# First MLP layer streams 32 instead of 64 columns per matmul; the useless matmuls of the layer norm become 512 columns wide

## The chip, the cores and the metric

The kernel runs on one core of a Trainium2 chip. The metric is the device time of one execution in microseconds (us); medians over executions are quoted.

PE is the matmul engine (PEld its weight loads), DVE the vector engine, ACT the scalar engine, SP the engine that issues most transfers, PSUM the memory that matmuls write to.

## The reference, cut to what matters

It is one decode step for 8 sequences: a modulated layer norm, attention over a cache of 8192 keys and values for 8 key/value heads, an output projection, then a second layer norm and an MLP. Only the part after the projection matters here:

```python
x = x + ga * attention(h, k_cache, v_cache, wq, wo)
h = _layernorm(x) * (1 + cb) + sb
hid = relu(h @ w1 + b1) ** 2          # 8 x 512 by 512 x 1792: "layer one"
x = x + gb * (hid @ w2 + b2)          # 8 x 1792 by 1792 x 512: "layer two"
```

## The kernel before: the parts that the change touches

Activations are held transposed, 128 features on the partitions and 8 sequences in the columns, so a matmul has only 8 useful columns. The kernel repeats them eight times (`wide`), 64 columns, so that PE has more to stream, and it puts matmuls of an identity matrix, whose result nobody reads, where PE would wait ("useless matmuls"). Neither touches the result; I take both to be there for the granted clock of PE, which in this kernel's trace is 1.0 or 0.5 of full speed. Full speed counts: back-to-back matmuls of 128 columns start 56 ns apart at 1.0 and 107 at 0.5.

```python
def pe_fill(n, at=7):                       # n useless matmuls of 128 columns
    for _ in range(n):
        op("tensor", lambda e: e.matmul(bank(at)[:, 0:128], IDENT[:, :], IDENT[:, :]))
def pe_stream(n, at):                       # n useless matmuls of 512 columns
    rhs = IDENT[:, :].unsqueeze(1).to_broadcast([128, 4, 128])
    for _ in range(n):
        op("tensor", lambda e: e.matmul(bank(at).rearrange("p (a r) -> p a r", a=4), IDENT[:, :], rhs))
# ... (cut: attention) ...
# the second weight matrix, 14 row tiles of 128, in two transfers: 12 tiles (1536 KB) and 2
d_w2 = [dma("sync", s_w2[i], lambda e, a=a, z=z, j=j: e.dma_start(
    W2v[:, a:z, :].rearrange("p (k j) n -> p k (j n)", j=j),
    B_w2[128 * a:128 * z].rearrange("(k p j) n -> p k (j n)", p=128, j=j)))
    for i, (a, z, j) in enumerate(((0, F2, 4), (F2, FT, 2)))]
# ... (cut) ...
# x1T is ready; mean by matmul, transposes of x1, then
pe_fill(4, 7)
# ... (cut: difference, squares, sum on DVE; variance by matmul; square root on ACT; h on DVE) ...
pe_fill(14, 7)
wcol = lambda k, f: fcol(W1v[:, k, :], f)   # every 4th column of W1 (every 2nd in the last two tiles)
for ks in (range(KT - 1), range(KT - 1, KT)):
    for f in range(FT):                     # layer one: 14 x 4 = 56 matmuls
        for k in ks:
            t = op("tensor", lambda e, f=f, k=k: e.matmul(
                hT_w[f // 7][:, f % 7, :, :], wcol(k, f), wide(hbT[:, k, :]), start=False, ...),
                [k_hb, d_w1[k // (KT - 1)]])
        # ... (cut: after f = 6 and f = 13, DVE: relu, square -> k_sq) ...
for f in range(FT):                         # layer two: 14 x 2 = 28 matmuls of 256 columns
    if f == F2:                             # F2 = 12
        pe_fill(6, 7)
    for cc in range(2):
        t = op("tensor", lambda e, f=f, cc=cc: e.matmul(
            yN_ps[64 * cc:64 * cc + B, :], hidT[:, f, :], W2v[:, f, 256 * cc:256 * (cc + 1)], ...),
            [k_sq[f // 7], d_w2[0 if f < F2 else 1]])
# ... (cut: two DVE operations, output) ...
```

## Time and profile before

672.04 us (median of 3, 671.46 to 672.15); the profiled execution took 671.61. The page of the profiled execution gives what bounds the kernel as a whole:

```profile
DMA  9999999999999999999999999999999999999995
...
HBM read 283.66 MB, written 0.01 MB: 423 GB/s over the span
```

The transfers are busy until the last 40th of the span: the kernel is bound by what it reads. Its tail, after the last values have landed at 656.50 us, is where the change lies. Here is the tail on PE, from the timeline: start in us, duration in us, engine, line, operation, output<-inputs, shapes, count; in brackets how long the engine was idle before, and whom it waited for.

```profile
657.48 0.96 PE L659 MATMUL PS<-oTn,wo_sb 128*128 128x8 bf16 x32 [0.29 <-DVE oTn L654]
...
659.95 0.39 PE L684 MATMUL PS<-sqs,ONESM 128*128 128x8 f32 x2 [0.21 <-DVE sqs L682]
660.19 1.04 PE L433 MATMUL PS<-IDENT 128*128 128x128 bf16 x14
661.38 3.12 PE L696 MATMUL PS<-hbT,ring 128*128 128x64 bf16 x56
664.82 1.48 PE L713 MATMUL PS<-ring,hidT 128*8 128x256 bf16 x24 [0.32 <-DVE KTb L702]
```

L632 is the last product with the values, L659 the last piece of the output projection, L684 the variance, L433 the useless matmuls, L696 layer one, L713 layer two. The chain that ended last, in order of time (start, duration, what):

```profile
656.55 0.66 PE PS L632 x16
...
661.38 2.81 PE PS L696 x49
...
664.47 0.22 DVE hidT L704
...
664.83 1.47 PE PS L713 x24
666.30 0.44 PE PS L433 x6
666.74 0.33 PE PS L713 x4
```

So layer one, ReLU, layer two, the six useless matmuls and the last four follow each other without a gap. The view of stretches gives the granted clock of PE in the first number after the groups (PEclk; then the DMA share and GB/s):

```profile
core 0: us, PE busy (x) PEld busy (x) DVE busy (x) ACT busy (x) POOL busy (x), PEclk, DMA share, GB/s
661.40:664.20 2.80, 2.80 (x53) 2.80 (x54) 0.00 (x0) 0.00 (x0) 0.00 (x0) 0.50 0.53 208
664.80:667.00 2.20, 2.18 (x34) 1.48 (x34) 0.23 (x2) 0.00 (x0) 0.00 (x0) 1.00 0.00 0
```

Layer one ran at half clock (0.50), 53 ns from start to start, layer two at full clock (1.00), 109 ns from one pair of matmuls to the next. The clock records of the trace have these two values alone and, from 36.25 us on, 37 switches between them, each a whole multiple of 3.41 us after the one before. The last two before the end of layer two are at 660.89 us, to half, and at 664.30, back to full. A "window" below is one such stretch of 3.41 us between two possible switches. And a last line, from the list of transfers (size in KB, us from issue to landing):

```profile
ring<-in_B_w_dram SPq DMA_DIRECT2D x1, 1536.0 KB, 24.5
```

This is the large part of the second weight matrix, issued at 640.14 us. The landing records of the trace show its 16 parts arriving from 660.96 to 664.69 us. Layer two needs all of them; `hidT`, its other input, was ready at 664.47 + 0.22 = 664.69 us.

### The profile page before, as it was taken

To read this page: it belongs to the slowest core of one execution; us is meant where nothing else is said; L and a number is where in the kernel's file an instruction comes from. 1 tells how busy PE (TensorE), PEld (TensorE's weight loads), DVE (VectorE), ACT (ScalarE), POOL (GpSimd) and SP (SyncE) were. 2 spreads that over 40 slices of the span, in tenths; PEclk is the share of its full clock that TensorE was granted. 3 is DMA by queue.
4 is the path that set the end of the run, shared out by engine and by line. 5 is a ranking of instruction groups with operands and counts; after the bars stand their busy time and mean duration, and the time that the engine had idled before them with its cause. 6 is when DMAs were issued, how large, how long until landed. Compare 5 with 4: busy or idle time off the path is not lost.

```text
span 669.9 us, 16178 instructions
## 1 busy us (share of the span) xinstructions
PE 496.0 (74%) x7486; PEld 342.4 (51%) x7486; DVE 299.4 (45%) x568; ACT 235.5 (35%) x281; POOL 17.2 (3%) x67
## 2 busy tenths in 40 slices
PE   2295964799639983699648995499836996489976
PEld 2283731676218751477317761287415763177644
DVE  2162741467216661267315671166503673156722
ACT  2052630466006640166204660066302652046600
POOL 7200000000000000000000000000000000000000
PEclk9996996799869997599958997699977999789998
DMA  9999999999999999999999999999999999999995
GB/s 373 435 399 434 429 425 436 433 427 434 430 436 430 425 432 434 436 430 427 430 436 432 429 431 429 436 434 427 432 429 438 433 429 425 434 438 434 425 412 235
DMA packets 12938, 283.96 MB, mean 424 GB/s; under 512 B 1234, under 2 KB 2291, under 8 KB 4340
## 3 DMA queue, kind: packets, MB, share of 16 engines
q1 hardware_dynamic: 12868, 283.65, 98.9%
q8 instruction: 13, 0.21, 0.1%
q14 instruction: 9, 0.07, 0.0%
q10 hardware_dynamic: 48, 0.02, 0.0%
HBM read 283.66 MB, written 0.01 MB: 423 GB/s over the span
## 4 chain that ended last, share of the span: by engine, by line
PE 50%; DMA 41%; DVE 5%; ACT 2%; issue 1%; SPq 0%
DMA ring<-in_A_k_cache_dram 37%; PE PS L447 36%; PE PS L462 9%; DMA ring<-in_A_v_cache_dram 4%; DVE Pm L552 3%; PE PS L580 2%; ACT KTb L452 1%; ACT P_sb L530 1%; DVE m L467 1%; PE PS L539 1%; PE PS L438 0%; PE PS L559 0%; PE PS L696 0%; PE PS L713 0%; DVE rhs_r L556 0%
## 5 line engine op out<-in xcount | busy, mean ns | idle before, releaser
L452 ACT ACTIVATE KTb<-PS 128x1024 bf16<-128x1024 bf16 x192 | 196.8, 1025 | 376.3 <-PE PS L447 376.3
L447 PE MATMUL PS<-IDENT,ring 128*128 128x128 bf16 x4096 | 266.4, 227 | 51.6 <-DMA ring<-in_A_k_cache_dram 43.7
L447 PEld LDWEIGHTS PS<-IDENT,ring 128*128 128x128 bf16 x4096 | 245.8, 102 | 100.4 <-DMA ring<-in_A_k_cache_dram 44.8
L454 DVE COPY KTb<-PS 128x1024 bf16<-128x1024 bf16 x320 | 209.9, 688 | 150.3 <-PE PS L447 148.3
L580 PE MATMUL PS<-ring,Pm 128*32 128x512 bf16 x992 | 81.1, 485 | 64.5 <-DMA ring<-in_A_v_cache_dram 63.6
L589 DVE CAST O_sb<-PS 128x512 bf16<-128x512 f32 x31 | 21.4, 692 | 144.0 <-PE PS L580 144.0
L462 PE MATMUL PS<-KTb,Qb 128*32 128x512 bf16 x1024 | 79.2, 386 | 4.5 <-ACT KTb L452 4.5
L580 PEld LDWEIGHTS PS<-ring,Pm 128*32 128x32 bf16 x992 | 29.2, 115 | 101.8 <-DMA ring<-in_A_v_cache_dram 65.0
L438 PE MATMUL PS<-IDENT 128*128 128x512 bf16 x120 | 31.3, 380 | 0.0
L530 ACT ACTIVATE P_sb<-PS,negm 128x512 bf16<-128x512 f32 x32 | 21.6, 686 | 18.9 <-DVE negm L526 18.9
L593 PEld LDWEIGHTS PS<-SEL,O_sb 128*128 128x128 bf16 x124 | 5.2, 98 | 44.8 <-DVE O_sb L589 44.8
L593 PE MATMUL PS<-SEL,O_sb 128*128 128x8 bf16 x124 | 8.0, 170 | 24.8 <-DVE O_sb L589 24.8
L462 PEld LDWEIGHTS PS<-KTb,Qb 128*32 128x32 bf16 x1024 | 15.5, 94 | 21.1 <-ACT KTb L452 8.5
L552 DVE COPY Pm<-PS 64x512 bf16<-64x512 bf16 x48 | 19.5, 419 | 13.4 <-PE PS L539 12.4
L467 DVE TENSOR_REDUCE m<-PS 128x1 f32<-128x512 f32 x32 | 22.1, 689 | 6.6 <-PE PS L462 6.6
L539 PE MATMUL PS<-IDENT,P_sb 128*64 128x128 bf16 x512 | 20.4, 222 | 2.0 <-ACT P_sb L530 1.2
L539 PEld LDWEIGHTS PS<-IDENT,P_sb 128*64 128x64 bf16 x512 | 15.2, 109 | 9.8 <-ACT P_sb L530 9.8
L438 PEld LDWEIGHTS PS<-IDENT 128*128 128x128 bf16 x120 | 9.9, 103 | 10.8 <-issue 3.4
L596 DVE TENSOR_TENSOR oTn<-PS,rinv 128x8 bf16<-128x8 f32 x31 | 6.0, 194 | 10.9 <-PE PS L593 10.9
L549 ACT ACTIVATE Pm<-PS 64x512 bf16<-64x512 bf16 x16 | 9.5, 593 | 1.1
L398 PE MATMUL PS<-haT,ring 128*128 128x8 bf16 x128 | 3.6, 168 | 7.0 <-DMA ring<-in_A_wq_dram 7.0
L686 ACT ACTIVATE std<-PS,epst 128x8 f32<-128x8 f32 x1 | 0.3, 268 | 23.1 <-PE PS L684 23.1
(116 smaller groups left out, 106.0 us busy)
## 6 DMA issues: line engine op xcount, KB each, us to landing
ring<-in_A_k_cache_dram SPq DMA_DIRECT2D x32, 4096.0 KB, 34.8
ring<-in_A_v_cache_dram SPq DMA_DIRECT2D x31, 4096.0 KB, 28.4
ring<-in_A_wq_dram SPq DMA_DIRECT2D x1, 4096.0 KB, 20.4
ring<-in_w_mod_dram SPq DMA_DIRECT2D x1, 3072.0 KB, 10.4
wo_sb<-in_A_wo_dram SPq DMA_DIRECT2D x1, 3072.0 KB, 45.1
ring<-in_A_v_cache_dram SPq DMA_DIRECT2D x1, 2048.0 KB, 23.2
ring<-in_B_w_dram SPq DMA_DIRECT2D x1, 1536.0 KB, 24.5
ring<-in_B_w_dram SPq DMA_DIRECT2D x1, 1344.0 KB, 20.7
```

What stands on the lines that cost most here:

```text
L438: op("tensor", lambda e: e.matmul(bank(at).rearrange("p (a r) -> p a r", a=4), IDENT[:, :], rhs))
L447: t = op("tensor", lambda e, j=j, i=i: e.matmul(STG[j][:, i, :], src[:, 32 * k + 8 * j + i, :], IDENT[:, :], is_transpose=True), [loaded[n ...
L452: stg_free[j] = op("scalar", lambda e, j=j, dst=dst: e.activation(dst, STG[j], ACT.Copy), [t], "scaP")
L454: stg_free[j] = op("vector", lambda e, j=j, dst=dst: e.tensor_copy(dst, STG[j]), [t], "vecP")
L462: t = op("tensor", lambda e, hf=hf, q=q, rhs=rhs: e.matmul(PS[32 * q:32 * (q + 1), k, :], Qb[:, 2 * p + hf, :], rhs, start=(p == 0 and hf ...
L467: return op("vector", lambda e: e.tensor_reduce(m4[:, k:k + 1], bank(k), AX.X, ALU.max), [t])
L530: exps.append(op("scalar", lambda e, k=k: e.activation(P_sb[:, k, :], bank(k), ACT.Exp, bias=negm[:, 0:1], scale=inv_sqrt, accum_out=rs4[: ...
L539: t = op("tensor", lambda e, k=k, i=i, hf=hf, src=src: e.matmul(STG[k][64 * hf:64 * (hf + 1), i, :], src, IDENT[:, :], is_transpose=True, ...
L552: done.append(op("vector", lambda e, dst=dst, frm=frm: e.tensor_copy(dst, frm), [t, k_pm], "vecP"))
L580: t = op("tensor", lambda e, p=p, m=m, cg=cg, vt=vt, Obank=Obank: e.matmul(Obank[32 * cg:32 * (cg + 1), :], lhs[:, p, 32 * m:32 * m + 32], ...
L589: t = op("vector", lambda e, osb=osb, Obank=Obank: e.tensor_copy(osb, Obank), [t], "vecP")
L593: t = op("tensor", lambda e, i=i, osb=osb, oT_ps=oT_ps: e.matmul(oT_ps, osb[:, i * 128:(i + 1) * 128], SEL[:, i, :], start=(i == 0), stop= ...
```

## The change

Its intent: keep PE's clock from falling in the layer norm, as it did at 660.89 us before, by useless matmuls that stream longer, and make layer one itself shorter.

```diff
-        wide = lambda ap: ap.unsqueeze(1).to_broadcast([128, 8, B])
+        wide = lambda ap, n=8: ap.unsqueeze(1).to_broadcast([128, n, B])
@@ after x1T is computed on DVE, before the mean @@
+        pe_stream(2, 7)
@@ after the transposes of x1 @@
-        pe_fill(4, 7)
+        pe_stream(2, 7)
@@ after the variance @@
-        pe_fill(14, 7)
+        pe_stream(3, 7)
@@ layer one @@
-    hT_w[f // 7][:, f % 7, :, :], wcol(k, f), wide(hbT[:, k, :]), ...
+    hT_w[f // 7][:, f % 7, 0:4, :], wcol(k, f), wide(hbT[:, k, :], 4), ...
@@ layer two, before the last four @@
             if f == F2:
-                pe_fill(6, 7)
+                pe_stream(1, 7)
```

The results stay the same: only the first of the repeated copies is read.

More of the change, by code (lines that the diff above doesn't have):

```diff
@@ L696, in bass_adaLN_cond__gqa_block_cached__dense_activation_squared_relu__decode_kernel @@
                     t = op("tensor", lambda e, f=f, k=k: e.matmul(
-                        hT_w[f // 7][:, f % 7, :, :], wcol(k, f), wide(hbT[:, k, :]), start=False, stop=(k == KT - 1),
+                        hT_w[f // 7][:, f % 7, 0:4, :], wcol(k, f), wide(hbT[:, k, :], 4), start=False, stop=(k == KT - 1),
                         skip_group_check=True), [k_hb, d_w1[k // (KT - 1)]])
```

## The prediction

> **What bounds the kernel now.** DMA: the page gives 283.66 MB of HBM reads at 423 GB/s over the 669.9 us span. The last part of the value cache lands at 656.50 us. Only the 13.4 us after that can be touched; the diff is all there.
>
> **The tail now (timeline, chain, windows).** Layer norm 658.47 to 661.34; first MLP layer (56 matmuls, 64 columns) 661.38 to 664.20 on the chain; ReLU and square until 664.69; second layer from 664.82 with six useless 128-column matmuls (0.44 us on the chain) before its last four.
> - The first layer runs at half clock: granted clock 0.50 from 660.9 to 664.3. Its start-to-start is 53.3 ns; the same shape in the output projection at full clock takes 31 ns.
> - [...] only 0.5 and 1.0, switching at multiples of 3.41 us. Counting streamed columns over clock per window, all windows after which full clock was lost had at most 0.34 busy, those that kept it at least 0.37; half clock ended after windows of at least 0.78, and stayed at up to 0.71. The window before the first layer had 0.34.
>
> **What the change does.** In the layer norm, 18 useless matmuls of 128 columns become seven of 512; in the last window that is about 1.5 us of streaming instead of 0.9, share about 0.53, so the clock should stay at 1.0 into the first layer. They fit into waits (0.43, 0.43, 0.64 us), delaying the chain by under 0.05 us. Layer one streams 32 columns: 25 to 30 ns apiece at full clock (estimate from the 25 ns of the 8-column projection), 27 to 33 at half clock (the first projections). It shrinks from 2.9 to about 1.6 us.
>
> **Why little of this arrives.** The large part of the second weight matrix (1536 KB, issued 640.14, 24.5 us to landing) lands at about 664.7, just when layer two starts today. So layer two cannot start more than about 0.1 us earlier; the 1.4 us become a wait for DMA. One 512-column matmul instead of six of 128 saves about 0.12 us. And PE now idles before layer two: the window holding layer one has only about 0.22 busy (1792 columns), below 0.34, so where a window ends shortly before or in layer two, that layer runs at half clock: up to +1.3 us. By replaying the tail with these shares for every window phase I get about -0.15 us in two thirds of the phases and +0.7 to +1.5 in a quarter to a third (at the profile's phase: +1.2).
>
> **Predicted:** 671.9 us (median), 671.1 to 673.2. Faster by 2% 0.005, same 0.985, slower 0.01.
>
> **What would show it.** Right: layer one about 1.5 us long; 1.0 clock during it; layer two's first weight load released by the DMA of the second MLP weight at about 664.7, with 1 us of idle PE before it; in some executions half clock in layer two (pairs of matmuls 213 instead of 109 ns apart) and a longer tail. Wrong: the second layer starting at 663.5; half clock still in layer one; useless matmuls delaying the mean or variance matmul by more than 0.1 us.
>
> **What would make it wrong.** A landing of the second weight matrix that shifts; a clock rule that counts weight loads too; window phases that are not random, so that the runs all fall in the bad third (about 673.1) or all in the good one.

671.9 agrees with before's 672.04 less the 0.15 us of most phases, and the upper end, 673.2, with 1.2 us more. The shares are an estimate of mine from before's trace: the time that a window's columns need at the pace of the trace (216 ns for 512 columns at full clock; 107 for 128 at half), overlaps counted once, over 3.41 us. A recount over its 186 windows gives up to 0.33 before the 19 losses of full clock, 0.37 and more in the 123 windows that kept it, 0.79 and more in the 18 that ended half clock, up to 0.71 in the 26 that did not.

## More of the kernel before

From the first matmul of the projection to the first of layer one it is 3.91 us; I call that the layer norm.

## The result, and the profile after

671.67 us (median of 4: 671.51, 671.66, 671.69, 673.11) against 671.93 us of before in the same series: the ratio is 1.0002 with a 95% interval of 0.9985 to 1.0019, so the same. (Ratios are the mean time of one kernel's fast runs over that of the other's fast runs of the same rounds, so not quite the ratio of the medians quoted.) Three executions are a little faster than before's median, one is 1.2 us slower.

The profiled execution of the changed kernel, the same views. Timeline of PE:

```profile
658.12 1.01 PE L659 MATMUL PS<-oTn,wo_sb 128*128 128x8 bf16 x32 [0.29 <-DVE oTn L654]
658.99 1.01 PE L438 MATMUL PS<-IDENT 128*128 128x512 bf16 x2
...
661.45 1.44 PE L438 MATMUL PS<-IDENT 128*128 128x512 bf16 x3
662.69 1.97 PE L697 MATMUL PS<-hbT,ring 128*128 128x32 bf16 x56
665.04 1.48 PE L714 MATMUL PS<-ring,hidT 128*8 128x256 bf16 x24 [0.38 <-DVE hidT L705]
```

Chain:

```profile
656.80 1.05 PE PS L632 x16
...
661.60 1.29 PE PS L438 x3
662.89 1.56 PE PS L697 x49
...
664.73 0.23 DVE hidT L705
...
665.04 1.48 PE PS L714 x24
666.52 0.32 PE PS L438
666.84 0.33 PE PS L714 x4
```

Stretches (layer norm, layer one, layer two):

```profile
658.00:662.30 4.30, 4.18 (x49) 2.35 (x49) 1.46 (x9) 0.65 (x3) 0.00 (x0) 0.50 0.95 378
662.70:664.40 1.70, 1.70 (x54) 1.70 (x54) 0.00 (x0) 0.00 (x0) 0.00 (x0) 0.75 0.33 125
665.00:667.00 2.00, 1.96 (x29) 1.24 (x29) 0.29 (x2) 0.00 (x0) 0.00 (x0) 1.00 0.00 1
```

Layer one became shorter: 1.80 us from its first to its last start, where it was 2.93. But this execution had half clock through the whole layer norm, and the 512-column matmuls are now on the chain (L438). The layer norm takes 662.69 - 658.12 = 4.57 us instead of 3.91. It also began 0.64 us later (658.12 against 657.48): the last values came 0.25 us later, and L632 took 1.05 us at half clock instead of 0.66. `hidT` is ready at 664.95 us, almost when the transfer lands (664.91 us by the landing records).

Which of the two released layer two can be read from a constant. In all eight traces here in which layer two waits for the undivided transfer, its first matmul starts 0.135 us after the landing (to within 1 ns in before and after; 0.14 in the chains of streams_only, narrow_only, after_fillwait, after_contig and after_nolast; in after_again the landing is read only to 0.1 us, and agrees), although `hidT` was ready between 0.09 and 1.50 us before that start. In the six traces without that wait (layer two without its transfer, or the transfer cut in pieces) it starts 0.05 us after `hidT` (664.64 and 664.69 in before_w2free, 663.86 and 663.92 in after_split). So the landing was the last input in the kernel before too, by about 0.08 us, and in this execution by about 0.04, although both chains name DVE there.

This is not the picture that the prediction drew (full clock, then a long wait for DMA): the landing sets the start of layer two, but nearly all of the long wait is missing, since `hidT` is late as well. The experiments had to tell which happens when.

### The profile page after: what moved, and what is told of

It reads as the page before. It is cut to its first block, busy times and chain, and to the rows that moved or that the text cites. A ratio compares the mean times of both kernels' runs of the same rounds, so it can differ in the third digit from the quotient of the medians.

```text
span 669.9 us, 16146 instructions
## 1 busy us (share of the span) xinstructions
PE 496.9 (74%) x7470; PEld 341.3 (51%) x7470; DVE 299.6 (45%) x568; ACT 235.3 (35%) x281; POOL 17.0 (3%) x67
## 4 chain that ended last, share of the span: by engine, by line
PE 51%; DMA 41%; DVE 5%; ACT 2%; issue 1%; SPq 0%
DMA ring<-in_A_k_cache_dram 37%; PE PS L447 36%; PE PS L462 9%; DMA ring<-in_A_v_cache_dram 4%; DVE Pm L552 3%; PE PS L580 2%; ACT KTb L452 1%; PE PS L438 1%; ACT P_sb L530 1%; DVE m L467 1%; PE PS L539 1%; PE PS L559 0%; PE PS L714 0%; DVE rhs_r L556 0%; DVE Dm L521 0%
## 5 line engine op out<-in xcount | busy, mean ns | idle before, releaser
L438 PE MATMUL PS<-IDENT 128*128 128x512 bf16 x128 | 35.1, 393 | 0.0
L552 DVE COPY Pm<-PS 64x512 bf16<-64x512 bf16 x48 | 19.5, 419 | 13.4 <-PE PS L539 12.4
L438 PEld LDWEIGHTS PS<-IDENT 128*128 128x128 bf16 x128 | 10.8, 105 | 11.5 <-issue 4.1
```

The costliest lines, as they stand in the source:

```text
L552: done.append(op("vector", lambda e, dst=dst, frm=frm: e.tensor_copy(dst, frm), [t, k_pm], "vecP"))
```

## The experiments

Theory A, the landing: layer two cannot start before its weights land at about 664.7 us, so a shorter layer one turns into waiting. Theory B, the clock: the switches of a trace lie on a grid of 3.41 us, and the grid lies differently from execution to execution (660.89 and 664.30 us in before's trace, 656.72 and 663.54 in after's), so which parts run at half clock differs too; and a layer one that streams little can lose full clock for layer two, since full clock was lost after windows with few columns in before's trace (0.33 and less). The second half is my estimate from those shares; what makes the clock switch no trace shows. Rival 1: the useless matmuls delay the layer norm and eat the gain. Rival 2: layer one does not really get shorter.

All times in one table; "before" is the median of the kernel before in the same series. The last columns come from the profiled execution only: the clock in the layer norm, layer one and layer two (F full, H half, m mixed), the time at which the first half of `hidT` is ready, and the first start of layer two, both in us.

| run | us: median (range), n | before | ratio, 95% interval | clock | hidT | layer two |
|---|---|---|---|---|---|---|
| before_w2free | 671.61 (670.47 to 672.15), 5 | 672.02 | 0.9992, 0.9979 to 1.0006 | F H m | 664.64 | 664.69 |
| after_w2free | 671.35 (670.73 to 671.64), 5 | 672.02 | 0.9991, 0.9977 to 1.0004 | H H m | 664.27 | 664.32 |
| narrow_only | 671.78 (671.74 to 673.58), 5 | 672.02 | 1.0003, 0.9989 to 1.0016 | m H H | 664.47 | 665.01 |
| streams_only | 671.55 (671.41 to 672.02), 5 | 672.02 | 0.9996, 0.9982 to 1.0009 | F F F | 663.69 | 664.81 |
| after_again | 671.54 (671.29 to 672.79), 5 | 671.76 | 1.0001, 0.9987 to 1.0014 | H m F | 664.58 | 664.68 |
| after_fillwait | 671.64 (671.63 to 671.78), 5 | 671.76 | 0.9997, 0.9983 to 1.0010 | F F F | 663.91 | 664.93 |
| after_split | 670.59 (670.34 to 671.08), 5 | 671.76 | 0.9982, 0.9969 to 0.9996 | F F F | 663.86 | 663.92 |
| wide_split | 671.04 (670.27 to 671.45), 5 | 671.76 | 0.9989, 0.9975 to 1.0002 | F F F | 663.77 | 663.83 |
| after_contig | 673.43, 1 (state unknown) | 671.82 | none | F F H | 663.73 | 665.24 |
| after_nolast | 672.01 (671.21 to 672.29), 5 | 671.82 | 0.9997, 0.9983 to 1.0011 | F F m | 664.10 | 665.09 |
| after_splitonly | 670.75 (670.53 to 671.43), 5 | 671.82 | 0.9983, 0.9970 to 0.9997 | H m F | 664.56 | 664.61 |
| narrow_split | 671.31 (670.59 to 671.56), 5 | 671.82 | 0.9988, 0.9974 to 1.0002 | m H H | 663.60 | 663.66 |

### 1 and 2: layer two without its transfer (wrong results on purpose)

The same edit in the kernel before and in the changed one. Layer two multiplies with the bytes of the first weight matrix, which have landed by then; the second is still loaded, and SP waits for it before it issues the output.

```diff
+        W2x = RING[:, s0, 0:FT * D].rearrange("p (f n) -> p f n", f=FT)    # the bytes of W1
-    yN_ps[...], hidT[:, f, :], W2v[:, f, ...],   [k_sq[f // 7], d_w2[0 if f < F2 else 1]])
+    yN_ps[...], hidT[:, f, :], W2x[:, f, ...],   [k_sq[f // 7], d_w1[1]])
+        Pg.wait("sync", d_w2)
```

> The kernel before, but the second layer multiplies with data of the first weight matrix (already landed, same shape) and so never waits for the second one; that is still loaded in full. Result wrong on purpose. If the second layer of the kernel before is bound by layer one and the landing together (both at 664.7 us), little is gained: -0.1 to -0.4 us against before. Rival (landing has nothing to do with it): 0.0. Both near, the pair with the next run decides.

> The changed kernel with the same edit, result wrong on purpose. Landing theory: the time that layer one saves now reaches the end, about -1.0 to -1.5 us against before where the changed kernel itself shows about 0. Rival 1 (the useless matmuls delay the layer norm and eat the gain) and rival 2 (layer one did not get shorter on average): within 0.3 us of the changed kernel, so about 0 against before.

Measured: 671.61 and 671.35 us against 672.02. The first is at the edge of what was expected; the second misses its range (-0.67 instead of -1.0 to -1.5 us), and only its fastest execution, 670.73, reaches -1.3. The two medians are 0.26 us apart with overlapping ranges, and both intervals contain 1, so by the times the pair decides nothing. A trace shows what happened in one execution of the second, of 671.12 us; three of the five were slower than that, and why is not shown. PE in the profiled execution:

```profile
658.28 1.01 PE L438 MATMUL PS<-IDENT 128*128 128x512 bf16 x2
...
660.74 1.44 PE L438 MATMUL PS<-IDENT 128*128 128x512 bf16 x3
661.97 2.01 PE L697 MATMUL PS<-hbT,ring 128*128 128x32 bf16 x56
664.32 1.58 PE L715 MATMUL PS<-ring,hidT 128*8 128x256 bf16 x24 [0.34 <-DVE hidT L705]
```

It again had half clock in the layer norm (4.54 us from the projection to layer one), so `hidT` was ready only at 664.27 us. Layer two did start 0.32 us before the transfer had landed (664.64 us), so the landing does bind, but by a third to half a microsecond in such an execution (0.46 with the 0.135 us that follow a landing). Theory A as I had put it, one long wait that swallows everything in every execution, falls, though the landing is the last input in all eight undivided traces. In the executions that run the layer norm at half clock, that delay takes part of the gain before the landing can (rival 1). Rival 2 falls: layer one got shorter in every trace with 32 columns.

### 3 and 4: each half of the change alone

narrow_only is the kernel before with the 32 columns; streams_only is the changed kernel with 64.

```diff
# narrow_only, against before
-    hT_w[f // 7][:, f % 7, :, :], wcol(k, f), wide(hbT[:, k, :]), ...
+    hT_w[f // 7][:, f % 7, 0:4, :], wcol(k, f), wide(hbT[:, k, :], 4), ...
# streams_only, against after: the same line the other way round
```

> The kernel before with only the 32-column first layer; useless matmuls as before. Landing theory with the clock rule [...]: layer one shorter, but no gain as the landing binds; in some executions half clock in layer two, so median -0.1 to +0.3, single executions +1.3 to +1.8 us. If a shorter layer one counts: -0.9 us or more.

> The changed kernel with the first layer at 64 columns again. Landing theory with the clock rule: -0.1 us median, no execution over +0.5 us, since the 64 columns keep the window busy. If the useless 512-column matmuls do the harm by delaying the layer norm: +0.3 us or more in the median, and the slow executions of about +1.3 us are here too.

Both came in kind as the clock theory had it; the medians lay a little lower than expected (-0.24 us where -0.1 to +0.3 was expected, -0.47 where -0.1 was). streams_only: PE, chain and stretch of layer one:

```profile
664.81 1.48 PE L714 MATMUL PS<-ring,hidT 128*8 128x256 bf16 x24 [1.40 <-DMA ring<-in_B_w_dram]
...
640.41 24.26 DMA ring<-in_B_w_dram
664.67 0.14 issue
664.81 1.48 PE PS L714 x24
...
661.40:663.30 1.90, 1.90 (x56) 1.88 (x56) 0.09 (x1) 0.00 (x0) 0.00 (x0) 1.00 0.63 244
```

With full clock kept, layer one with 64 columns takes 1.83 us from first to last start, 1.1 us less than before without any narrowing, and the layer norm takes 3.91 us, exactly what it took before. `hidT` was ready at 663.69 us; then PE waited 1.40 us for the transfer, and the chain leads into it. Theory A holds in this execution: the gain is there, and the landing takes it.

narrow_only had two executions of five at 673.22 and 673.58 us, and the profiler caught one of them:

```profile
664.88 0.14 issue
665.01 2.72 PE PS L713 x24
...
665.00:669.00 4.00, 3.99 (x34) 2.10 (x34) 0.00 (x0) 0.00 (x0) 0.00 (x0) 0.50 0.00 0
```

Layer two ran at half clock: 213 ns from one pair of matmuls to the next, where all full-clock traces have 109. From its first start to the start of the two DVE operations behind it it took 669.05 - 665.01 = 4.04 us, where before took 2.28. That and the 0.19 us by which it started later (665.01 against 664.82) are the slow execution in full. Full clock had gone at 659.04 us already, in the layer norm, and did not come back over layer one with 32 columns; in before's trace it was lost at 660.89 and came back at 664.30, after layer one with 64.

### 5 and 6: more executions, and the wait filled

after_again is the changed kernel, unedited. after_fillwait has three useless matmuls more, where PE waits for the transfer:

```diff
+        pe_stream(3, 7)
         for f in range(FT):      # layer two
```

> The changed kernel, unedited, for more executions. Clock theory: most within 0.5 us of before or a little faster, and where a window ends between layer one and layer two, one that loses full clock there and is 1.2 to 1.6 us longer (as one of four was, 673.1). Rival (that slow execution was chance of the DMA): no trace and no time of this kind comes again.

> The changed kernel with three useless 512-column matmuls more, between layer one and layer two, where PE idles for the second weight matrix. Clock theory: [...] no execution loses full clock in layer two, so none over before's longest by more than 0.3 us; median as the changed kernel's fast ones, -0.1 to -0.4 against before. Rival (layer two starts late for another reason): slow ones remain, or all get 0.2 to 0.6 us longer as the filling delays layer two.

after_again gave one long execution of five, 672.79 us; with the first series, two of nine executions of the changed kernel are over 672.5 us, and the longest of the 31 executions of before was 672.42. None of the five with the wait filled was over 671.78. That is what theory B expects, though five executions without a slow one are weak evidence by themselves: with two in nine, about three such fives in ten would have none ((7/9)^5 = 0.28). In the profiled one, the wait for the transfer after the filling was still 0.65 us, and layer two ran at full clock:

```profile
664.93 1.48 PE L715 MATMUL PS<-ring,hidT 128*8 128x256 bf16 x24 [0.65 <-DMA ring<-in_B_w_dram]
```

### 7, 8, 11 and 12: the transfer in smaller pieces

If the landing takes the gain, layer two should start on what has already landed. The large transfer is cut in three, each with its own semaphore, same bytes in the same order:

```diff
-            s_w2 = [sem(f"d_w2{i}") for i in range(2)]
+            s_w2 = [sem(f"d_w2{i}") for i in range(4)]
-            ... enumerate(((0, F2, 4), (F2, FT, 2)))]
+            ... enumerate(((0, 4, 4), (4, 8, 4), (8, F2, 4), (F2, FT, 2)))]
-            [k_sq[f // 7], d_w2[0 if f < F2 else 1]])
+            [k_sq[f // 7], d_w2[f // 4]])
# after_split, wide_split and narrow_split also leave out the useless work before the last four:
-            if f == F2:
-                pe_stream(1, 7)        # (pe_fill(6, 7) in narrow_split)
```

after_split is the changed kernel with both edits, after_splitonly with the first alone; wide_split has 64 columns in layer one; narrow_split has the 128-column useless matmuls of before in the layer norm.

> The changed kernel with the second weight matrix loaded in pieces of 4, 4, 4 and 2 row tiles with a semaphore each (was 12 and 2), and without the useless matmul before the last four. Landing theory: layer two starts when layer one is done (663.5 to 664.3), only its last pairs wait for 664.7 and 665.3, so -0.9 to -1.5 us against before. If the landing is not what binds: -0.2 us from the useless matmul left out.

> As the run before this, but with the first layer at 64 columns. Where the layer norm kept full clock, layer one takes 1.7 instead of 1.5 us and layer two still hides in the landing: about the same as the 32 columns; where it did not, layer one takes 2.9 us and the end is 0.7 to 1.0 us later. Mean 0.2 to 0.5 us behind the 32-column version, -0.5 to -1.2 us against before.

> The changed kernel with only the finer loading of the second weight matrix (the useless matmul before the last four stays). Landing theory: most of the 1.2 us that the two edits together gave is from this one: -0.8 to -1.1 us against before; the useless matmul then fits in the wait for the last piece and costs 0.0 to 0.2 us.

> As the best one so far (finer loading, no useless matmul before the last four, 32 columns), but with the narrow 128-column useless matmuls of the kernel before in the layer norm. Layer one takes 33 ns per matmul at either clock, so the useless matmuls matter only through their delay at half clock and through layer two's clock: within 0.3 us of the best one; single executions up to 1.3 us longer if layer two loses full clock.

after_split: 670.59 us against 671.76, the ratio's interval below 1, and its slowest execution (671.08) is faster than the fastest of before (671.54) and of the unedited changed kernel (671.29) in that series. Chain of its profiled execution:

```profile
661.61 1.76 PE PS L697 x49
...
663.64 0.23 DVE hidT L705
663.87 0.04 issue
663.92 1.62 PE PS L712 x24
665.53 0.03 issue
665.57 0.41 PE PS L712 x4
```

Layer two starts 0.05 us after `hidT` is ready; the pieces landed at 662.41, 663.63, 664.89 and 665.52 us, and two short waits are left, 0.14 us for the third piece and about 0.2 before the last four matmuls (665.57). after_splitonly gives nearly all of it, 670.75 against 671.82; its profiled execution, with half clock in the layer norm, is the slowest of its five (671.43). So the finer loading was worth about 0.95 us (after_split against the unedited changed kernel of its series, 671.54; perhaps 0.1 of it is the useless matmul left out), which neither half of the change could reach. The kernel before with the finer loading alone was not run, so how much of the 1.1 us against before needs the change is open. wide_split and narrow_split, 671.04 and 671.31, lie between; their intervals overlap with after_split's, so which of the layer norms and widths is best is not settled. narrow_split missed its expectation: it is 0.72 us behind after_split and not within 0.3. Its trace shows half clock all through both layers (layer two's 28 matmuls took 3.15 us, against 1.93 in wide_split).

### 9: the weights of layer one side by side (wrong result)

All traces with 32 columns had 33 ns from start to start in layer one, at full and at half clock (after has both in one layer: 33 until 663.54 us, 33 behind it), and those with 64 columns had 33 at full clock (streams_only) and 53 at half (before). So 33 ns is not the streaming. What differs from the other projections is that `wcol` reads every fourth column as weights.

```diff
-        wcol = lambda k, f: fcol(W1v[:, k, :], f)
+        wcol = lambda k, f: W1v[:, k, 128 * f:128 * (f + 1)]
```

> The changed kernel with the weight columns of layer one read side by side instead of every fourth (every second for the last two tiles); result wrong on purpose. So far layer one has 33 ns from start to start at full and at half clock with 32 columns, and 33 ns at full clock with 64. If the strided read of the weights sets that, it falls to 25 to 27 ns here, as in the other projections; if not, it stays at 33 ns. Time of the kernel: unchanged within 0.5 us either way, as the landing binds.

```profile
661.83 1.57 PE L697 MATMUL PS<-hbT,ring 128*128 128x32 bf16 x56 [0.39 <-DVE hbT L690]
665.24 2.72 PE L714 MATMUL PS<-ring,hidT 128*8 128x256 bf16 x24 [1.83 <-DMA ring<-in_B_w_dram]
```

The distance fell to 25 ns, the weight loads from a median of 118 ns each (117 or 118 in the traces of after, after_again, streams_only, narrow_only, after_split and after_w2free) to 95 (after_contig): in this kernel the strided read sets the 33 ns (shown at full clock; at half clock this was not run). The time of the one execution, of unknown state, was not within 0.5 us, as I had expected: it was 673.43. Layer one was over at 663.4 us, PE waited 1.83 us for the transfer, and layer two then ran at half clock, pairs 213 ns apart. It is theory B's bad case in the changed kernel, with layer one even a little shorter.

### 10: without the useless matmul before the last four

```diff
-            if f == F2:
-                pe_stream(1, 7)
```

> The changed kernel without the one useless 512-column matmul before the last four of layer two. It stands on the chain for about 0.33 us (from the trace: 0.32 us from its start to the next one's at full clock), so -0.2 to -0.4 us against the changed kernel, about -0.5 against before in the executions that keep full clock. If it is needed to keep the clock: no gain.

Two of the five executions, 671.21 and 671.26, are faster than every unedited one (671.29 and up); the other three are 672.01 to 672.29. In the profiled one (672.25), full clock was lost at 665.75, in the middle of layer two. The unedited changed kernel was not run in this series. The expected gain is not shown in the median, and whether leaving the matmul out invites the loss or these were chance window positions stays open.

## Why the prediction was right, point by point

The time was right: 671.67 us, in the range and 0.2 from the forecast, "same". That says little by itself: before's own median lies in the range, and the whole tail is 13.4 of 672 us. The bound named, the landing, holds in every trace; the way to it was another one in both profiled executions of the changed kernel, and that the median came so close is in part luck.

- **"layer two cannot start more than about 0.1 us earlier; the 1.4 us become a wait for DMA".** The first half is right in all eight traces with the undivided transfer: layer two starts 0.135 us after the landing, at 664.68 to 665.24 us, where before had 664.82. The second half is right where the layer norm keeps full clock: PE waits 1.40 us (streams_only), 0.65 us after the filling (after_fillwait) and 1.83 us (after_contig), and the split of the transfer brings about 0.95 us back. The sign that I named, 1 us of idle PE before layer two, is absent from the profiled execution of the changed kernel and from after_again's, since their layer norm was at half clock and `hidT` was late by itself. Two of the signs that I had named for "wrong" are there instead: half clock in the first part of layer one, until 663.54 us, and useless matmuls that delay the mean and the variance matmul by 0.15 and 0.33 us.
- **"the clock should stay at 1.0 into the first layer".** It did in the six profiled executions with 512-column useless matmuls whose layer norm began at full clock (the first two of these matmuls took 0.59 us, against 1.01 at half clock); after_w2free, which lost it at 657.73 us, 0.3 us into the projection and before the first of these matmuls, is not counted. I had argued from the one window position of before's profile. In the two profiled executions of the changed kernel full clock was already lost before the layer norm, in a window that the change does not reach.
- **"They fit into waits ... delaying the chain by under 0.05 us".** Right at full clock: 3.91 us from projection to layer one in before and in streams_only. Wrong at half clock: 4.57 us (after, after_again, after_splitonly), 0.66 more, with the useless matmuls on the chain. How long before's own layer norm is when it runs at half clock throughout, no trace shows. narrow_only, with the same useless matmuls as before and half clock in most of it, had 4.38, so not all of the 0.66 can be put on the wider ones.
- **"25 to 30 ns apiece at full clock, 27 to 33 at half clock".** It is 33 ns at both, because of the strided weights (shown at full clock): 1.80 us and not "about 1.6". What 32 columns buy is a layer one that does not mind half clock, 33 instead of 53 ns; at full clock they buy nothing (33 and 33).
- **"-0.15 us in two thirds of the phases and +0.7 to +1.5 in a quarter to a third".** Seven of nine executions of the changed kernel lie between 671.29 and 671.77, two at 672.79 and 673.11. Half clock in layer two was caught in narrow_only, narrow_split and after_contig, and from its middle on in after_nolast; no profile of the unedited changed kernel caught it, so for its two slow executions it is inferred.
- **The shares, "at most 0.34" and "at least 0.37".** They describe one trace and are not shown to be limits. The same count on the trace of the changed kernel (after, 185 windows) has full clock lost after up to 0.32 busy and kept from 0.42, half clock ended from 0.81 and staying up to 0.75, where the forecast had 0.71. after_nolast lost full clock after a window (662.34 to 665.75 us) of about 0.35, an estimate from its timeline: some 40 matmuls of 32 columns and 0.66 us of layer two. The streamed columns go with the switches in these traces; that they alone decide them is not shown. Nor does it take useless matmuls to get full clock back: in before's trace PE ran only transposes of keys (32 of 128x128) from 121.6 to 125.0 us, and the granted clock was 0.50 there and 1.00 from 125.10 to 128.30.
- **"One 512-column matmul instead of six of 128 saves about 0.12 us".** 0.32 instead of 0.44 us on the chain: right.

## What to carry to other kernels

Before shortening a stage that feeds another, look for the other inputs of that next stage and their landing times: a chain names one input only, and here, with a second one within 0.01 us of it, not the one that released the stage. Which one releases the stage showed here in a delay that stays the same from trace to trace (0.135 us after the landing, 0.05 after `hidT`). Where the transfer is the one, cutting it into pieces with a semaphore each can be worth more than a faster engine, as it was here (about 0.95 us). A shorter stage followed by a wait can cost the stage behind it: in after_contig the granted clock was 1.00 in layer one (661.8 to 663.3 us) and, after a wait of 1.83 us, 0.50 in layer two (665.3 to 668.6 us), with pairs of matmuls 213 instead of 109 ns apart. So measure several executions and look at the clock of each trace before comparing them.
